# Three product widths in place of four in the expert stage of an attention, experts and MLP kernel

## The chip, the cores and the metric

The kernel runs on one core of a Trainium2 chip. The metric is the device time of one execution in microseconds (us), taken as the median of several executions. The profile is of one more execution of the same program.

## The reference

Three layers follow each other. What concerns the change is the second one, and of it the two matrix products per expert:

```python
def _moe_ref(x, expert_emb, tau, w1, w2):        # x: 2304 tokens x 512
    logits = xn @ en.T / tau                     # en: 8 experts
    expert_idx = np.argmax(logits, axis=1)
    ...
    for e in range(E):                           # E = 8
        mask = expert_idx == e
        h = np.maximum(x[mask] @ w1[e], 0.0)     # 512 -> 1024
        out[mask] = gate_w[mask, None] * (h @ w2[e])   # 1024 -> 512

def reference(...):
    attn_out = _attn_ref(q, k, v, w_phi)         # linear attention, 4 x 8 heads x 576 x 64
    x = _moe_ref(x=tokens of attn_out, ...)
    return _moe2_ref(x, w1, w2, w3, w_out)       # max of three products with 512 x 768, then 768 x 512
```

How many tokens an expert gets depends on the data, and differs from expert to expert. With these inputs the eight experts get 291, 494, 122, 198, 430, 296, 283 and 190 tokens.

## The kernel before

The kernel has three stages, one after the other on one core: the attention (until about 217 us of the profile), the experts (217.6 to 463.3 us) and the last MLP (from 463.3 us). All code is unrolled; each engine has one fixed sequence of instructions, written in the order in which the Python code issues them, and engines wait for each other through semaphores.

Attention ends with the routing (class `Routing`): each token's expert by an argmax, the tokens counted by expert (`ne`, line 732), and for each expert the number of the thresholds in `th` that its count exceeds (`cmp`, line 735, and the sum into `vi`). `th` is filled on GpSimd at line 658 from `WIDTHS` without its last entry. So `vi` holds for each expert the index of the smallest width that holds all its tokens. A count over `CAP` = 512 is dealt with by another path (`redo`), which these inputs jump over.

The experts stage (`Mlps.experts`) loops over the eight experts. Tokens stand as columns, sorted by expert, so an expert's tokens are a range of columns that starts at an offset known only at run time. The first product of an expert is cut into eight units (`A`, f = 0 to 7; line 987), each of 12 matmuls into one PSUM bank: four pieces of 128 input features, with three terms each, since inputs and weights are split into a high and a low part. The second is cut into four units (`B`, d = 0 to 3; line 1006) of 24 matmuls each. So an expert has 8 x 12 + 4 x 24 = 192 matmuls.

The number of columns of a matmul is fixed in its instruction. So each unit is written once for every width (`pick`, line 958 on): the index is in a register of TensorE (one load for each expert, line 1023), compare-and-branch instructions of TensorE's own sequencer (line 966) choose one of the copies, and the other copies are jumped over. `pick` halves the list of widths: with four, two compares choose. A width N multiplies the first N columns from the offset on; columns beyond the expert's own tokens are computed and later overwritten or left out.

With these counts the eight experts take the widths 304, 512, 224, 224, 448, 304, 304 and 224, in this order.

What the other engines do in a unit does not depend on the width: ScalarE and VectorE read 512 columns of the bank always (lines 994, 995 and 1009). Between the units they split the next expert's weights into high and low part (`split_w`; lines 849 and 854 for the first product, 957 and 958 for the second), after which SyncE loads the weights of a later expert into the same buffer (line 861). For expert 0 alone the first unit of `A` also brings in tokens (`first`): there ScalarE and VectorE branch too.

Of the kernel before, what the change touches and what calls it, by code (L numbers as in the profile page):

```python
# [617 lines left out]
class Routing:  # L618


    WIDTHS, CAP = (224, 304, 448, 512), 512

    def __init__(self, tc, gp, rp, NT, E):
        self.tc, self.nc, self.gp, self.rp = tc, tc.nc, gp, rp
# [780 lines left out]
```

## Time and profile before

| | |
|---|---|
| median of 3 runs | 770.54 us (770.53, 770.54 and 772.1) |
| the profiled execution | 771.95 us |
| its span, first to last instruction | 770.2 us |
| TensorE (PE) busy | 733.9 us, 95% |
| VectorE (DVE), ScalarE (ACT), GpSimd (POOL) busy | 403.9, 353.9 and 136.1 us |
| mean granted TensorE clock | 0.989 of 2.4 GHz |
| experts stage in the profile | 217.6 to 463.3 us |

The profile names work by engine and line of the code. A busy share is an average over stages with different limits. A row of the timeline ends, where the engine was idle before it, with the idle time in us and what ended it; "issue" there is time in which the engine waited for nothing that the profile shows. Branches, register loads and waits run on an engine's sequencer ("PEldq" for TensorE's), which runs ahead of the array, and don't count as busy. The queue "instruction" among the DMA queues carries the program's own code.

### The profile page before, as it was taken

How to read it: one execution, taken by the hardware profiler on the slowest of the kernel's cores; microseconds unless marked ns; L12 is line 12 of the kernel's file. 1: busy time of each engine (PE TensorE's matmuls, PEld its weight loads, DVE VectorE, ACT ScalarE, POOL GpSimd, SP SyncE). 2: the span in 40 equal slices, each digit the busy share in tenths (PEclk: the TensorE clock that was granted, in tenths of full speed). 3: DMA queues.
4: the chain of work that ended last, by engine and by line, in shares of the span. 5: the costliest groups of instructions: out<-in, count | busy, mean ns of one | idle time of the engine just before them, and what ended most of it. 6: DMA issues, size and time to landing. Idle time of an engine off the chain costs nothing. (4 is left out here: it accounts for less than half of the span.)

```text
span 770.2 us, 13409 instructions
## 1 busy us (share of the span) xinstructions
PE 733.9 (95%) x5492; PEld 607.6 (79%) x5492; DVE 403.9 (52%) x619; ACT 353.9 (46%) x600; POOL 136.1 (18%) x113
## 2 busy tenths in 40 slices
PE   8899999899998999898999998999999999999995
PEld 6566666665698889898999997888888887888884
DVE  7876666777765454484455678766522122212220
ACT  4676757676665445574455575343230131013111
POOL 1654223442151101004700000000020011002002
PEclk9899999999999999999999999999999999999999
DMA  9644433026248442454423605432010001001001
GB/s 202 141 102 99 115 89 83 18 83 221 81 131 302 162 168 80 172 170 116 162 108 118 220 9 164 161 119 102 2 54 28 1 23 36 0 1 56 0 1 55
DMA packets 59755, 76.15 MB, mean 99 GB/s; under 512 B 11632, under 2 KB 41976, under 8 KB 59648
## 3 DMA queue, kind: packets, MB, share of 16 engines
q1 hardware_dynamic: 55712, 64.53, 27.0%
q0 software_dynamic: 3456, 9.46, 3.6%
q8 instruction: 83, 1.36, 0.8%
q10 hardware_dynamic: 480, 0.61, 0.2%
q14 instruction: 24, 0.20, 0.1%
HBM read 65.12 MB, written 9.46 MB: 97 GB/s over the span
## 5 line engine op out<-in xcount | busy, mean ns | idle before, releaser
L1260 DVE TENSOR_TENSOR raw<-raw,b 128x512 f32<-128x512 f32 x36 | 24.8, 688 | 130.6 <-PE b L1252 126.8
L341 POOL PARTITION_ALL_REDUCE mq<-pq x32 | 69.0, 2207 | 98.0 <-ACT pq L339 91.3
L1006 PE MATMUL b<-hxH,wH 128*128 128x304 f32 (+3 forms) x256 | 80.1, 313 | 3.5 <-issue 3.5
L1281 POOL DMA_INDIRECT out_dram<-raw,c2t x18 | 17.8, 988 | 363.9 <-ACT raw L1280 334.5
L995 DVE SCALAR_TENSOR_TENSOR hxL<-b,hxH 128x512 fp32r<-128x512 f32 x64 | 42.4, 687 | 75.1 <-ACT hxH L994 74.8
L1006 PE MATMUL b<-hxL,wH 128*128 128x304 f32 (+3 forms) x256 | 79.4, 310 | 0.0
L1006 PE MATMUL b<-hxH,wL 128*128 128x304 f32 (+3 forms) x256 | 79.2, 309 | 0.0
L994 ACT ACTIVATE hxH<-b 128x512 fp32r<-128x512 f32 x64 | 38.4, 607 | 51.6 <-PE b L987 51.6
L987 PE MATMUL b<-xeH,w1lo 128*128 128x304 f32 (+3 forms) x256 | 56.8, 317 | 4.9 <-issue 4.9
L987 PE MATMUL b<-xeH,w1hi 128*128 128x304 f32 (+3 forms) x256 | 56.4, 313 | 0.0
L1006 PEld LDWEIGHTS b<-hxH,wH 128*128 128x128 f32 x256 | 48.4, 189 | 6.6 <-issue 4.9
L1006 PEld LDWEIGHTS b<-hxL,wH 128*128 128x128 f32 x256 | 48.5, 189 | 1.8
L1006 PEld LDWEIGHTS b<-hxH,wL 128*128 128x128 f32 x256 | 48.4, 189 | 1.7
L987 PEld LDWEIGHTS b<-xeH,w1lo 128*128 128x128 f32 x256 | 43.4, 195 | 7.5 <-issue 5.4
L987 PEld LDWEIGHTS b<-xeH,w1hi 128*128 128x128 f32 x256 | 42.0, 189 | 1.6
L958 DVE TENSOR_TENSOR wL<-raw,wH 128x2048 fp32r<-128x2048 f32 x16 | 36.7, 2294 | 11.4 <-ACT wH L957 11.4
L987 PE MATMUL b<-xeL,w1lo 128*128 128x304 f32 (+3 forms) x128 | 39.9, 316 | 0.0
L987 PE MATMUL b<-xeL,w1hi 128*128 128x304 f32 (+3 forms) x128 | 39.8, 311 | 0.0
L927 POOL DMA_INDIRECT xs<-x_d,s2t x18 | 21.9, 1215 | 101.3 <-PE b L933 71.1
L1264 ACT CAST m2h<-raw 128x512 fp32r<-128x512 f32 x12 | 7.4, 620 | 67.8 <-DVE raw L1260 67.8
L228 DVE TENSOR_REDUCE mk<-pskp 128x4 f32<-128x512 f32 x36 | 24.6, 684 | 24.9 <-PE pskp L217 24.9
L1009 ACT COPY xy<-b 128x512 f32 (+1 forms) x32 | 18.0, 587 | 42.1 <-PE b L1006 41.8
(254 smaller groups left out, 1786.7 us busy)
## 6 DMA issues: line engine op xcount, KB each, us to landing
raw<-in_moe_w_dram SPq DMA_DIRECT2D x32, 1024.0 KB, 5.8
raw<-in_moe_w_dram SPq DMA_DIRECT2D x18, 512.0 KB, 3.5
q<-in_q_dram SPq DMA_DIRECT2D x8, 576.0 KB
kv<-in_v_dram SPq DMA_DIRECT2D x8, 512.0 KB, 7.3
x_d<-x SPq DMA_DIRECT2D x16, 256.0 KB, 2.1
kv<-in_k_dram SPq DMA_DIRECT2D x7, 512.0 KB, 5.5
raw<-in_moe_w_out_dram SPq DMA_DIRECT2D x6, 512.0 KB, 4.8
kv<-in_k_dram SPq DMA_DIRECT2D x2, 256.0 KB
```

Of the source, the lines that this page charges most:

```text
L228: nc.vector.tensor_reduce(m, psb[j], axis=AX.X, op=ALU.max, apply_absolute_value=True)
L341: nc.gpsimd.partition_all_reduce(mx.rearrange("p a b -> p (a b)"), d.rearrange("p a b -> p (a b)"), P, ReduceOp.absmax)
L927: self.nc.gpsimd.indirect_dma_start(out=d, out_offset=None, in_=self.x_d, in_offset=bass.IndirectOffsetOnAxis(ap=idx, axis=0))
L958: self.nc.vector.tensor_tensor(L, r, H.bitcast(F32), op=ALU.subtract)
L987: nc.tensor.matmul(ps[:, 0:N], w, x[:, k, 0:N], start=(i == 0), stop=(i == 11))
L994: nc.scalar.activation(hH, ps, AF.Relu)
L995: nc.vector.scalar_tensor_tensor(hL, ps, 0.0, hH.bitcast(F32), op0=ALU.max, op1=ALU.subtract)
L1006: nc.tensor.matmul(ps[:, 0:N], w[i][:, c:c + P], h[f // 4][:, f % 4, 0:N], start=(f == 0 and q == 0), stop=(f == 7 and q == 2))
L1009: nc.scalar.copy(self.xy[:, d, bass.ds(o, 512)], ps)
L1260: nc.vector.tensor_tensor(m, m, b, op=ALU.max)
L1264: nc.scalar.copy(hH, m)
L1281: nc.gpsimd.indirect_dma_start(out=self.out, out_offset=bass.IndirectOffsetOnAxis(ap=rt.c2t[:, t:t + 1], axis=0), in_=o, in_offset=None)
```

## The change

One line: the width 448 is taken out of the list, and three widths are left.

```diff
 class Routing:
...
-    WIDTHS, CAP = (224, 304, 448, 512), 512
+    WIDTHS, CAP = (224, 304, 512), 512
```

Everything else follows from it. `th` has two thresholds in place of three (one small fill on GpSimd less, and `cmp` has 16 values in place of 24). Expert 4 (430 tokens) takes 512 columns in place of 448. `pick` halves three widths into one and two: one compare leads to 224, a second one tells 304 from 512.

On TensorE each unit loses one copy. This is the first unit of the second product of expert 0 in the program before (a unit of 24 matmuls; three of each copy shown, and b, hxH, hxL, wH, wL are the PSUM bank, the two parts of the hidden layer and of the weights):

```order
L966 COMPARE_AND_BRANCH x2
L1006 MATMUL b_2885<-hxH_2880,wH_2874 128x224
...
L966 UNCONDITIONAL_BRANCH
L1006 MATMUL b_2885<-hxH_2880,wH_2874 128x304
...
L966 UNCONDITIONAL_BRANCH
L966 COMPARE_AND_BRANCH
L1006 MATMUL b_2885<-hxH_2880,wH_2874 128x448
...
L966 UNCONDITIONAL_BRANCH
L1006 MATMUL b_2885<-hxH_2880,wH_2874 128x512
```

and in the changed program:

```order
L966 COMPARE_AND_BRANCH
L1006 MATMUL b_2884<-hxH_2879,wH_2873 128x224
...
L966 UNCONDITIONAL_BRANCH
L966 COMPARE_AND_BRANCH
L1006 MATMUL b_2884<-hxH_2879,wH_2873 128x304
...
L966 UNCONDITIONAL_BRANCH
L1006 MATMUL b_2884<-hxH_2879,wH_2873 128x512
```

Three copies of 24 matmuls stand in a row where four stood, with one compare and one jump less. The units of the first product change in the same way, with 12 matmuls a copy. The order of the work on the other engines is the same, but for one copy less of the two token blocks that ScalarE and VectorE bring in with expert 0.

## Rows read from the trace of the kernel before

**Rows 1.** Page: busy time of the engines; code queue (packets, MB, share).

```profile
PE 733.9 (95%) x5492; PEld 607.6 (79%) x5492; DVE 403.9 (52%) x619; ACT 353.9 (46%) x600; POOL 136.1 (18%) x113
...
q8 instruction: 83, 1.36, 0.8%
```

**Rows 2.** Busy time by stretch, one for each expert, in order.

```profile
core 0: us, PE busy (x) PEld busy (x) DVE busy (x) ACT busy (x) POOL busy (x), PEclk, DMA share, GB/s
217.60:249.10 31.50, 29.34 (x213) 28.81 (x213) 19.88 (x25) 19.56 (x27) 7.92 (x7) 1.00 0.63 222
249.10:294.70 45.60, 45.60 (x211) 37.67 (x210) 19.56 (x30) 18.23 (x23) 4.98 (x4) 1.00 0.42 150
294.70:319.20 24.50, 23.62 (x209) 23.26 (x208) 16.91 (x17) 17.93 (x24) 3.42 (x2) 1.00 0.44 160
319.20:349.10 29.90, 25.05 (x202) 24.25 (x200) 17.14 (x18) 17.35 (x22) 0.00 (x0) 0.94 0.50 172
349.10:388.10 39.00, 38.96 (x192) 36.14 (x193) 16.84 (x15) 15.63 (x18) 22.04 (x18) 1.00 0.36 113
388.10:414.60 26.50, 26.50 (x194) 26.49 (x193) 16.40 (x15) 15.95 (x19) 0.00 (x0) 1.00 0.41 147
...
441.10:463.30 22.20, 21.65 (x193) 21.48 (x193) 16.42 (x16) 14.69 (x17) 0.00 (x0) 1.00 0.13 44
```

**Rows 3.** TensorE's waits in the experts stage: us in total, times, longest.

```profile
PE b L987 <- issue: 4.9, 3, 2.3
PE b L1006 <- issue: 3.5, 6, 1.4
```

**Rows 4.** Timeline of TensorE: matmuls with idle time before them, and what ended it.

```profile
241.40 0.41 PE L1006 MATMUL b<-hxH,wH 128*128 128x304 f32 x1 [1.42 <-issue]
...
245.72 0.41 PE L1006 MATMUL b<-hxH,wH 128*128 128x304 f32 x1 [0.75 <-issue]
...
323.39 0.49 PE L987 MATMUL b<-xeH,w1lo 128*128 128x224 f32 x2 [2.34 <-issue]
...
340.96 0.36 PE L1006 MATMUL b<-hxH,wH 128*128 128x224 f32 x1 [0.20 <-issue]
...
344.15 0.36 PE L1006 MATMUL b<-hxH,wH 128*128 128x224 f32 x1 [0.26 <-issue]
...
349.14 0.46 PE L987 MATMUL b<-xeH,w1lo 128*128 128x448 f32 x1 [2.05 <-issue]
...
445.83 0.36 PE L987 MATMUL b<-xeH,w1lo 128*128 128x224 f32 x1 [0.55 <-issue]
```

**Rows 5.** Line 966 in the experts stage: duration in ns, least, median and longest.

```profile
L966 PEldq COMPARE_BRANCH  x274: 65/176/3571, 218.5 to 461.3; - x137
```

**Rows 6.** DMA: code queue (packets, MB, share), 217 to 464 us; GB/s of expert 0.

```profile
q8 instruction: 50, 0.82, 1.4%
...
GB/s 198 172 255 36 94 239 125 208 0 21 0 0 0 0 36 283 408 354 401 297 364 377 406 440 416 408 419 401 395 416 411 349 99 42 0 0 0 114 270 416
```

**Rows 7.** Line 1006 alone, in experts 1 (512 columns) and 4 (448 columns).

```profile
272.77:294.67 21.90, 21.90 (x96) 17.92 (x96) 1.00 0.31 111
368.69:388.14 19.45, 19.45 (x96) 17.84 (x95) 1.00 0.32 112
```

**Rows 8.** Busy time by stretch, as in rows 2, before and after the idle 2.34 us.

```profile
319.20:323.40 4.20, 1.86 (x18) 1.78 (x17) 0.69 (x1) 1.19 (x2) 0.00 (x0) 1.00 0.54 215
323.40:326.90 3.50, 3.50 (x18) 3.50 (x17) 0.69 (x1) 1.48 (x2) 0.00 (x0) 0.51 0.02 5
```

**Rows 9.** Timeline: the split of first-product weights; expert 1's first product.

```profile
245.97 1.23 DVE L854 TENSOR_TENSOR w1lo<-raw,w1lo 128x1024 fp32r<-128x1024 f32 x1
...
249.14 0.62 PE L987 MATMUL b<-xeH,w1lo 128*128 128x512 f32 x2
...
342.02 1.22 DVE L854 TENSOR_TENSOR w1lo<-raw,w1lo 128x1024 fp32r<-128x1024 f32 x1
```

**Rows 10.** Timeline of TensorE: the first wait in the last MLP.

```profile
470.83 0.50 PE L1252 MATMUL b<-xeH,w1lo 128*128 128x512 f32 x1 [1.86 <-ACT xy L1256]
```

## The prediction, made before the changed kernel ran

> **What bounds the kernel now.** I read the page first. TensorE (PE) is busy 733.9 of 770.2 us and its matmuls and weight loads are equal in number, so each product takes two instructions [rows 1]. The question is then what TensorE does in the experts stage, the only one whose instructions change. The stretches by expert say how long each takes: 31.5, 45.6, 24.5, 29.9, 39.0 and 26.5 us for experts 0 to 5, and 22.2 for expert 7 [rows 2]. From them comes the pace of a matmul with its weight load: expert 5 at 304 columns takes 26.50 / 192 = 138 ns, expert 7 at 224 columns 21.65 busy us / 192 = 113 ns. Experts 2 and 3 have the same 192 matmuls of 224 columns as expert 7, and 17 and 10 others beside them, yet take 24.5 and 29.9 us. The waits tell why: in the whole stage TensorE waits for no data worth naming, but nine times for "issue", 4.9 us before the first product and 3.5 us before the second, 8.4 us together [rows 3]. Seven of the nine are shown [rows 4]; the other two, at 310.14 and 313.77 us, are the rest, 0.9 us. Most lie in experts 2 and 3 and at the border to expert 4, the two largest are 2.34 and 2.05 us.
>
> What is it that "issue" hides? The reader should put the branches beside it. A compare-and-branch or jump of line 966 lasts 176 ns in the median and 65 at least, but 3571 at most [rows 5]: a branch that leads into code which hasn't come yet takes microseconds. The code queue brought 50 packets in the stage, 0.82 MB, so 16 KB each [rows 6]. The stage has 8 experts x (8 units x 12 + 4 units x 24) matmuls x 4 copies x 2 instructions = 12,288 instructions, 246 for each packet. So all four copies are fetched, those that are jumped over too, and a packet feeds 246 / 96 = 2.56 units of the first product or 246 / 192 = 1.28 of the second: in both 30.75 executed matmuls. At 224 columns that is 30.75 x 113 = 3.5 us of work per packet, at 304 columns 4.2 us. The stalls at 340.96 and 344.15 us, one unit apart [rows 4], show what a packet takes when the engine has to wait for each: 3.2 us. At 224 columns code arrives hardly faster than it is used up, and any packet that is late stops the engine. At 304 columns it stopped only where the weight loads keep the DMA engines at some 400 GB/s (227 to 243 us, [rows 6]): 1.42 and 0.75 us in expert 0, none in expert 5.
>
> **Part one: the 448-column expert at 512 columns.** Expert 4's second product took 19.45 us for 96 matmuls, 202.6 ns each; expert 1's, at 512 columns, 21.90 us for 96, 228.1 ns [rows 7]. The difference, 25.5 ns, times 192 matmuls is **+4.9 us**, all on the path, since expert 4 has no wait inside it. ScalarE and VectorE read 512 columns either way, and have idle time here (busy 15.6 and 16.8 of 39 us [rows 2]). The Trainium skill, "TensorE: Matmul & The Clock Gate", section "Back-to-back issue gap", gives a sustained spacing of about 81 ns at 128 and 131 ns at 512 columns; my estimate from that page is 50 / 384 ns per column, 1.6 us for this part, by which the sum below would come out 3.3 us lower. The rows differ (228 ns at 512), and they decide.
>
> **Part two: a quarter less code.** The stage has 9,216 instructions in place of 12,288, so at 246 a packet some 37 to 38 packets in place of 50. A packet then feeds 41 executed matmuls, not 30.75: 4.6 us at 224 columns, 5.7 us at 304. Against the 3.2 us that a packet takes this is a slack of 1.4 us where 0.3 us was. What goes is bounded from both sides. If each wait loses only what one packet now covers more (10.25 matmuls, 1.16 us at 224 and 1.41 us at 304), of the nine waits 0.01 + 1.18 + 0.89 = 2.1 us stay: 6.3 us are gained. If the slack adds up from packet to packet, as TensorE's sequencer runs ahead and stores it up, all 8.4 us are gained. I take 0.4 us as what stays, near the second end, because expert 5, with 4.2 us per packet, already shows no wait at all [rows 2], and the changed program has more than that everywhere: **-8.0 us**. A wait of 2 us or more can come back where a packet is held up behind weight loads; that is the other end, and I keep it for the range.
>
> **Part three: the clock.** After the 2.34 us wait the granted clock is 0.51 for 3.5 us, 1.2 GHz in place of 2.4 [rows 8]. In these 3.5 us 18 matmuls ran, which at 113 ns take 2.0 us: 1.5 us lost. The waits of 1.42, 2.05 and 1.86 us [rows 4, 10] were followed by no such drop (the stretch of expert 4 has 1.00 [rows 2]). If the longest wait shrinks below these, the drop goes too: **-1.5 us**.
>
> **Part four: branches and small things.** Three experts at 224 columns have 12 units each with one compare less, 36 in all. The sequencer runs ahead, and in expert 5, with 12 units to choose, no idle time shows, so I cost this at nothing; were that cover gone, it would be 36 x 65 ns = 2.3 us of gain. One small fill on GpSimd less and a shorter compare on VectorE lie far from the stage: nothing.
>
> **What is late next.** Faster products reach the next expert's weights sooner. Expert 1 would start 2.2 us earlier, at about 247.0 us; the low part of its second weight block is done at 245.97 + 1.23 = 247.2 us [rows 9], and the first matmul that reads it is the eighth, 7 x 228 ns = 1.6 us in. The margin is 1.4 us. Before expert 4 the same step ends at 343.2 us while TensorE came at 349.14; it depends on TensorE's own earlier steps and moves forward with them. The wait of 1.86 us at the start of the last MLP [rows 10] is for ScalarE, whose work there starts from expert 7's results and moves along too; it stays.
>
> **The sum.** 771.95 + 4.9 - 8.0 - 1.5 = 767.35 us against the profiled execution. That one is 1.4 us above the median of 770.54. Part of the difference may be waits for code that fell out shorter in the other runs, part lies elsewhere; I split it, and subtract 0.7: **766.6 us**, 0.5% below the median. Less or more than 1.5 us, 0.2%, is about what a measurement can tell from no change.
>
> **The rivals.** *Half of the waits stay* (chance 0.14). If packets are late mainly because weight loads hold them up, the waits are set by when loads run, not by how much code is asked for. For it: the waits of expert 0 under full DMA load. Against it: expert 5 loads weights too (147 GB/s on average [rows 2]) and doesn't wait. With 4.2 us and the clock drop kept: 771.95 + 4.9 - 4.2 = 772.65, less 0.7 to 1.4 for the median: 771.6, no change that can be told.
>
> *All of the waits stay, and the path only grows* (chance 0.05). The place is the same nine waits; the price is 4.9 us. It holds if a jump into the next packet always costs its fetch, however long ago the previous one came: then fewer packets mean fewer waits only by a quarter, 2.1 us at most, and the clock drop stays. The time is between 770.54 + 4.9 - 2.1 = 773.3 and 775.4. It decides slower from the point where less than 3.4 us of the 9.9 is regained. Against it: expert 5 jumps just as often and shows no idle time [rows 2]. The Trainium skill speaks for it in one sentence of "Runtime: NRT & Kernel Launch", section "Instruction fetch mechanics": crossing a block of code is "mostly hidden", so that less code would buy nothing and 4.9 us would be added, 775.4 us; the 8.4 us of "issue" disagree [rows 3]. The same section says that a branch out of the fetched window must wait for a fetch, and with that the longest branch, 3571 ns, agrees [rows 5].
>
> *The next weights are late* (chance 0.08). If expert 1's weights use up the margin of 1.4 us, the 2.2 us regained in expert 0 become a wait for data, at most 2.2 us: up to 768.8 us, still faster.
>
> **How the numbers follow.** My forecast holds with 0.73. Its own range: at the low end all waits go, and with them the whole 1.4 us, 771.95 + 4.9 - 8.4 - 1.5 - 1.4 = 765.5; a further 0.7 is kept for expert 0, whose 31.5 us less 2.2 us of waits are still 2.8 us more than expert 5's, not all of it in its 20 other matmuls. At the high end 2.1 us of waits stay and nothing of the 1.4 us goes: 769.05. To hold 8 in 10 the range reaches some way into the half-stays case: **764.8 to 769.8 us**. Faster by over 0.2% (below 769.0): 0.73 + 0.08 and a little of the first rival, 0.82. Within: 0.12. Slower (above 772.1): 0.06.
>
> **What would show it.** In the profile of the changed kernel: some 37 to 38 packets in the code queue in the stage and some 70 in all; "issue" before lines 987 and 1006 well under 2 us; no branch of line 966 much over 1.5 us in experts 2, 3 and 7; a granted clock of 1.00 in expert 3, and that expert near 24 us; expert 4 at 43.9 us with 192 matmuls of 512 columns; the last MLP as long as before. Four or more us of "issue" would prove the prediction wrong at part two, idle time at expert 1's start with VectorE as releaser at the margin, and an expert 4 much under 43 us at part one.

## The result and the profile after

The changed kernel takes 762.07 us in the median of six runs (759.82 to 766.39), beside 771.5 us for the kernel before in runs of the same chip (six, 770.53 to 776.88). The ratio is 0.987, with a 95% interval of 0.984 to 0.991. A later comparison with twelve runs gave 763.12 us against 771.66 us, 0.990 (0.988 to 0.993). So the change saves some 8 to 9 us, 1.0 to 1.3%. The direction was forecast, the size was not: the forecast was 766.6 us, in a range of 764.8 to 769.8.

The profiled execution of the changed kernel took 762.83 us with a span of 761.1 us; the one before took 771.95 and 770.2. The page shows the same work on TensorE and thirteen packets of code less [rows 1]:

```profile
PE 734.4 (96%) x5492; PEld 605.0 (79%) x5492; DVE 403.4 (53%) x619; ACT 353.4 (46%) x600; POOL 135.6 (18%) x112
...
q8 instruction: 70, 1.15, 0.7%
```

The stretches by expert answer to [rows 2]; the columns are the same:

```profile
216.90:245.70 28.80, 28.80 (x213) 28.80 (x214) 16.99 (x19) 17.37 (x24) 7.81 (x7) 1.00 0.63 220
245.70:291.20 45.50, 45.50 (x210) 37.61 (x210) 22.38 (x36) 20.32 (x27) 4.97 (x4) 1.00 0.46 163
291.20:314.30 23.10, 23.10 (x209) 23.10 (x208) 16.92 (x17) 16.59 (x22) 3.41 (x2) 1.00 0.43 144
314.30:336.70 22.40, 22.40 (x202) 22.33 (x202) 16.96 (x18) 17.76 (x24) 0.00 (x0) 1.00 0.55 192
336.70:380.30 43.60, 43.60 (x194) 36.09 (x194) 16.83 (x15) 16.31 (x19) 21.67 (x18) 1.00 0.44 132
380.30:406.80 26.50, 26.50 (x194) 26.48 (x193) 16.40 (x15) 15.96 (x19) 0.00 (x0) 1.00 0.43 148
...
433.20:455.10 21.90, 21.90 (x194) 21.56 (x193) 16.75 (x17) 14.56 (x17) 0.00 (x0) 1.00 0.15 52
```

In every stretch shown TensorE is busy from end to end. Against before, expert 0 is 2.7 us shorter, expert 1 0.1, expert 2 1.4, expert 3 7.5 and expert 7 0.3: 12.0 us together. Expert 4, now at 512 columns, is 4.6 us longer; expert 5 is the same. The stage takes 7.4 us less.

In the experts stage there is no row of "issue" at all, where [rows 3] had 8.4 us; the waits of TensorE that come next lie at the start of the last MLP (first fence below). Branches of nearly two microseconds still exist (line 966 in the whole program, compare [rows 5]), but no idle time stands behind them: the longest lasts from 319.04 to 320.94 us, and all through it TensorE works off matmuls of the units before. The code queue brings 37 packets in the stage (last fence), where [rows 6] had 50:

```profile
PE b L1252 <- ACT xy L1256: 1.4, 1, 1.4
PE b L1252 <- DVE xy L1260: 0.5, 1, 0.5
```

```profile
L966 PEldq COMPARE_BRANCH  x228: 70/176/1897, 213.6 to 453.2; - x114
```

```profile
q8 instruction: 37, 0.61, 1.2%
```

The other 1.6 us between the two spans lie outside the stage: 0.7 us before it, where the granted clock of the first 36 us was 0.95 in this execution and 0.91 in the earlier one, and 0.9 us after it, half of which is the wait for ScalarE, 1.38 us in place of 1.86 [rows 10]. The first of these differs from execution to execution: in a second profile of the changed kernel the clock of the first 36 us was 1.00, and the stage began at 214.6 us in place of 216.9.

### The profile page after: what moved, and what is told of

Read it like the earlier page. It is cut to its first block, busy times and chain, and to the rows that moved or that the text cites. A ratio compares the mean times of both kernels' runs of the same rounds, so it can differ in the third digit from the quotient of the medians.

```text
span 761.1 us, 13360 instructions
## 1 busy us (share of the span) xinstructions
PE 734.4 (96%) x5492; PEld 605.0 (79%) x5492; DVE 403.4 (53%) x619; ACT 353.4 (46%) x600; POOL 135.6 (18%) x112
## 5 line engine op out<-in xcount | busy, mean ns | idle before, releaser
L1006 PE MATMUL b<-hxH,wL 128*128 128x304 f32 (+2 forms) x256 | 80.3, 313 | 0.0
L1006 PE MATMUL b<-hxH,wH 128*128 128x304 f32 (+2 forms) x256 | 80.2, 313 | 0.0
L1006 PE MATMUL b<-hxL,wH 128*128 128x304 f32 (+2 forms) x256 | 80.0, 313 | 0.0
L987 PE MATMUL b<-xeH,w1hi 128*128 128x304 f32 (+2 forms) x256 | 57.2, 317 | 0.0
L987 PE MATMUL b<-xeH,w1lo 128*128 128x304 f32 (+2 forms) x256 | 55.7, 313 | 0.0
L987 PE MATMUL b<-xeL,w1hi 128*128 128x304 f32 (+2 forms) x128 | 40.1, 313 | 0.0
L987 PE MATMUL b<-xeL,w1lo 128*128 128x304 f32 (+2 forms) x128 | 39.5, 312 | 0.0
L1252 PE MATMUL b<-xeH,wH 128*128 128x512 f32 x96 | 37.3, 389 | 0.0
```

Source lines behind the costliest of these rows:

```text
L987: nc.tensor.matmul(ps[:, 0:N], w, x[:, k, 0:N], start=(i == 0), stop=(i == 11))
L1006: nc.tensor.matmul(ps[:, 0:N], w[i][:, c:c + P], h[f // 4][:, f % 4, 0:N], start=(f == 0 and q == 0), stop=(f == 7 and q == 2))
L1252: nc.tensor.matmul(b, w, y[k], start=(k == 0 and q == 0), stop=(k == 3 and q == 2))
```

## The experiments

Each run was timed against the kernel before on the same chip, whose median in these comparisons was 771.2 to 771.7 us.

**As much code as before, with the new columns.**

```diff
-    WIDTHS, CAP = (224, 304, 448, 512), 512
+    WIDTHS, CAP = (224, 304, 512, 512), 512
```

> Widths 224, 304, 512 and 512 again: the columns of the changed kernel, with as much code as before (the fourth copy is never run). If the gain is code that no longer has to be fetched, the nine waits of before come back and 512 columns still cost 4.6 us: 774 to 779 us, some 50 packets in the code queue in the experts stage, 'issue' of 5 us or more. If the gain comes from anything else that goes with three widths (columns, thresholds, VectorE's and ScalarE's shares), it stays near 762 us.

It took 776.03 us (ten runs, 772.45 to 778.39), 1.0054 of the kernel before (1.0032 to 1.0076). The code queue has 50 packets in the stage again, and the waits are back:

```profile
q8 instruction: 50, 0.82, 1.4%
...
PE b L987 <- issue: 5.0, 3, 2.9
PE b L1006 <- issue: 3.7, 5, 1.8
```

Expert 4 has the columns of the changed kernel here, and the copies, the packets and the compares are as many as before. So the new columns are not the gain: it goes with the fourth copy, be it by its code or by the compare that it adds to a unit of 224 columns. The run without weight loads below tells these two apart. The difference to the kernel before is the price of the wider expert, 4.2 us by these medians (2.5 to 5.9), 4.6 us by the stretches above.

**A quarter more code, with the old columns.**

```diff
-    WIDTHS, CAP = (224, 304, 448, 512), 512
+    WIDTHS, CAP = (224, 304, 384, 448, 512), 512
```

> Widths 224, 304, 384, 448 and 512: every expert takes the columns of before, with a quarter more code. A packet then feeds 24.6 matmuls, 2.8 us at 224 columns, less than the 3.2 us that a packet takes when it is waited for. If code supply sets the waits, they grow to 20 us or more in the experts stage: 783 to 800 us. If the waits depend on the number of branches or on the weight loads alone, the time stays within 770 to 775 us.

It took 797.66 us (793.27 to 802.77), 1.0356 (1.0308 to 1.0404). No expert has between 304 and 384 tokens, so the fifth copy is never run, and it costs 26 us. There are 63 packets in the stage, and "issue" adds up to 20.6 us:

```profile
q8 instruction: 63, 1.03, 1.6%
...
PE b L987 <- issue: 12.3, 7, 3.3
PE b L1006 <- issue: 4.8, 7, 1.8
PE b L933 <- issue: 3.5, 1, 3.5
```

Dead code costs what it delays, and the cost is far from proportional: 13 packets more cost 26 us, 13 less save some 12.

**Half the code.**

```diff
-    WIDTHS, CAP = (224, 304, 512), 512
+    WIDTHS, CAP = (304, 512), 512
```

> Widths 304 and 512: two copies of each unit, half the code of before, and the three experts that ran at 224 columns run at 304: 3 x 192 x 25 ns = 14.4 us more matmul time. If the changed kernel has no wait for code left, there is nothing further to regain: 762 + 14.4 = 776 to 777 us. If some of its time is still lost to code, 774 us or less.

It took 776.55 us (774.24 to 777.99), as expected. Its stage lasts 252.8 us in the profile, 14.5 more than the changed kernel's 238.3, as much as its three experts at 304 columns need. No branch of line 966 lasts over 0.35 us any more, and that brings nothing further:

```profile
L966 PEldq COMPARE_BRANCH  x168: 70/174/348, 213.3 to 466.0; - x168
```

So with three copies the supply of code is no longer on the path.

**The kernel before without weight loads.** This run leaves out the loads of the weights of experts 2 to 7, so that these experts are computed with the weights of expert 1.

```diff
-                    if e + 1 < E:
+                    if e == 0:
                         ex.load(2 + f // 2, e + 1)
...
-                    if e + 2 < E:
-                        ex.load(i, e + 2)
-                    else:
+                    if e + 2 >= E:
                         self.load_m2(i)
```

> The kernel before, but the weights of experts 2 to 7 are never loaded (expert 1's are used again): the experts stage without 24 of its weight transfers, with the same code. If packets are late because weight transfers hold them up, 'issue' falls from 8.4 to under 3 us and the time to about 762 us. If the plain rate of the code queue sets the waits, 'issue' stays above 6 us and the time above 768 us.

It took 765.2 us (763.69 to 767.44), 0.9912 (0.9884 to 0.994). "Issue" is halved, not gone:

```profile
PE b L987 <- issue: 2.3, 2, 2.0
PE b L1006 <- issue: 2.1, 3, 1.5
```

The 1.5 us wait, with one of 0.4 us after it, lies in expert 0, beside which expert 1's weights are still loaded (242.56 us; 1.42 us at 241.40 before [rows 4]). The 2.0 us wait lies at 350.59 us, in expert 4, and is followed by a clock of 0.50. Within experts 2 and 3 only 0.2 us is left, and 0.3 at the border to expert 4, where 2.05 was. So four copies of code would nearly have sufficed, had nothing else moved; it takes both the code and the loads beside it. My expectation of under 3 us was missed (4.4), and the time lies 3 us over the 762 that I gave; the places speak for the loads. How a load makes a packet late stays open: the transfers of the code packets take 1.1 us each on average with the loads and without them (1.4% of 16 engines over 247 us for 50 packets [rows 6]; 1.5% over 248 us for 52 here).

This run also settles what a compare costs. Expert 2's second product has four copies here and two compares in each unit; with no wait in it, it takes as long as in the changed kernel with three copies and one compare, 10.79 us:

```profile
307.84:318.63 10.79, 10.79 (x100) 10.79 (x97) 8.45 (x9) 7.10 (x9) 0.00 (x0) 1.00 0.11 30
```

So the compares are free here, and what the fourth copy costs it costs by its code.

**Four widths in one product, three in the other.** `pick` gets the list of widths as an argument; in these runs one product gets `(224, 304, 512)` and the other all four.

```diff
-    def pick(self, idx, unit, lo=0, hi=None):
-        W = self.rt.WIDTHS
+    def pick(self, idx, unit, lo=0, hi=None, W=None):
+        W = W or self.rt.WIDTHS
...
-        self.pick(idx, unit) if idx is not None else unit(512)
+        self.pick(idx, unit, W=(224, 304, 512)) if idx is not None else unit(512)
```

With three in the second product:

> Four widths in the first product, three in the second: a unit of the first product has the code of before, one of the second that of the changed kernel; expert 4 runs its first product at 448 columns and its second at 512, so half of the 4.6 us is saved. If a packet must be matched with the work that it feeds, the waits of the second product go and some of those of the first stay: 762 to 768 us. If waits of the first product stay as long as before (4.9 us and their overlap), 768 us or more.

It took 764.02 us (762.66 to 772.36), as expected, with 1.8 us of "issue". What expert 4's first product saves at 448 columns, the waits take back: no better than the changed kernel, within the spread. With three in the first product:

> Three widths in the first product, four in the second: the counterpart of the run with four and three. If each packet must be matched with the work that it feeds, the waits before the second product come back (3.5 us of idle and 1.5 to 2 us of overlap lost in six waits) and those before the first go: 762 + 5 - 2.3 = 764 to 766 us. If waits belong to the first product and the border between experts, it falls to 760 us.

It took 773.73 us (768.44 to 776.25), some 8 us over what I expected. That is 1.0028 of the kernel before (1.0001 to 1.0054), although that one has more code; it has 2.3 us less matmul time in expert 4. The waits of this run are 9.4 us:

```profile
PE b L1006 <- issue: 4.7, 7, 1.3
PE b L987 <- issue: 4.5, 2, 2.5
PE b L933 <- issue: 0.2, 1, 0.2
```

After the two longest of them the granted clock fell too: its mean was 0.87 in the 13.3 us from 320.48 us on and 0.94 in expert 4's first product, a further part of the 8 us. By my count of matmuls per packet the two runs should have differed little: the executed 224-column work per packet is 3.5 us in either product with four copies. What differs is what else moves. In this run the stretch of expert 2's first product and that of its second read:

```profile
293.32:305.69 12.37, 12.37 (x114) 12.37 (x112) 8.46 (x9) 9.53 (x14) 3.41 (x2) 1.00 0.28 96
305.69:320.48 14.79, 11.46 (x100) 10.93 (x97) 8.45 (x9) 8.97 (x12) 0.00 (x0) 1.00 0.66 242
```

The last two columns are the share of the DMA engines and GB/s: the next weights are loaded mainly beside the second product, 242 GB/s against 96. So I took the loads out of this run too, in the same way as above:

> The run with three widths in the first and four in the second product, without the weight loads of experts 2 to 7. The weight loads run mainly beside the second product, and the waits of that run lie in it and right after it. If it is the weight loads beside the four-copy second product that make packets late, its waits in experts 2 to 4 (some 10 us with the clock's share) go: about 763 us. If four copies of 24 matmuls are too much code whatever else moves, it stays above 770 us.

It took 765.33 us (760.33 to 768.76), 8.4 us less, but 2 us over what I expected: of the 2.6 us of "issue" that are left, 2.0 lie in expert 0, where expert 1's weights still come. The same two stretches are

```profile
294.56:306.93 12.37, 12.37 (x114) 12.37 (x112) 8.46 (x9) 9.53 (x14) 3.41 (x2) 1.00 0.08 24
306.93:317.72 10.79, 10.79 (x100) 10.79 (x98) 8.46 (x9) 7.09 (x9) 0.00 (x0) 1.00 0.11 30
```

The second product of expert 2 falls from 14.79 to 10.79 us, with the same code, and the loads are what was taken away. So the second product's fourth copy is the dear one because its code must come while the weights come; the counterpart, loads moved beside the first product, was not tried.

**Second profiles.** The kernel before, once more:

> The kernel before once more, unchanged, for a second profile. If the waits depend on when packets land among other transfers, their places and sizes differ from the first profile, with a sum between 6 and 12 us of 'issue' in the experts stage; if they are fixed by the code alone, the same nine places and 8.4 us come again.

It took 770.08 us in its one run. Its waits in the stage are

```profile
PE b L1006 <- issue: 3.6, 5, 1.8
PE b L987 <- issue: 3.0, 2, 2.3
PE b L987 <- ACT xy L1009: 1.4, 1, 1.4
PE b L1006 <- ACT xeH L946: 0.3, 1, 0.3
PE b L987 <- ACT hxH L994: 0.3, 1, 0.3
```

All nine places of the first profile are there again with other sizes: 1.81 and 0.37 us in expert 0 where 1.42 and 0.75 were, and 1.36 at the border to expert 4 where 2.05 was; the one at 344.15 us shrank to 0.10. Two are new, 0.3 us each in expert 3, where the first profile had half the clock instead after its wait of 2.34 us. The last three rows bear ScalarE's name. The wait at the border was "issue" in the first profile and goes with the code, so the name beside a wait need not be its cause; whether the two new ones are waits for code too is not shown. So the places come mostly from the code, and the sizes differ from execution to execution. Each half of my expectation held in part: the sum of "issue", 6.6 us, lies in the range, but the places did not move. The changed kernel once more:

> The changed kernel once more, for a second profile and for a comparison on one chip with the run at 496 columns: 760 to 764 us, and again no 'issue' before lines 987 and 1006 if the slack per packet is what counts; one or two waits of up to 1 us if the first profile was a lucky one.

It took 763.12 us (760.61 to 765.71) and has no "issue" in the stage again, which lasts 238.3 us in both profiles. So the first profile was not an exception.

**A smaller largest width.**

```diff
-    WIDTHS, CAP = (224, 304, 512), 512
+    WIDTHS, CAP = (224, 304, 496), 496
```

> The changed kernel with 496 in place of 512 as its largest width (494 is the largest count; more than 496 tokens would go the other path): the same code, and 16 columns less in the 384 matmuls of experts 1 and 4. At the 0.38 to 0.4 ns per column that 448 against 512 gave (24 to 25.5 ns for 64), 384 x 16 x 0.39 = 2.4 us less: 759 to 760 us. If the weight load sets the pace and not the columns, no change from 762 us.

It took 763.05 us (757.93 to 764.3), which is no gain by the medians. Expert 4's second product takes 21.44 us for 96 matmuls in its profile, 223 ns each, where the changed kernel takes 21.76 us, 227 ns:

```profile
353.97:375.41 21.44, 21.44 (x96) 17.88 (x95) 1.00 0.31 100
```

That is 4 ns x 384 = 1.5 us less for the two experts, and the stage lasts 236.8 us where the changed kernel's lasts 238.3. So a matmul's time does go by its columns, and not by the weight load alone. Beside the changed kernel on the same chip:

> The kernel with 496 as its largest width once more, beside the changed kernel: the first profile shows 223 ns for a matmul where 512 columns take 227, so 384 x 4 = 1.5 us less than the changed kernel. If that is real the medians differ by 1 to 2 us; the spread of single runs is larger than that, so it may not show.

This time it took 761.17 us against 763.12, 0.988 of the kernel before (0.984 to 0.993) against 0.990 (0.988 to 0.993). The intervals overlap, so whether this version beats the changed one in the time of a whole execution stays open; it also sends counts of 497 to 512, which the changed kernel holds, the other path.

## Why the prediction was wrong

**What bounds the kernel** was read rightly. Waits for code are what "issue" hid: with the columns of the changed kernel a fourth copy brings them back, and with the columns of before a fifth multiplies them. One figure in it was less sure than it looked. The 3.2 us that a packet takes came from two waits one unit apart; a unit is 24 matmuls, while a packet feeds 30.75, so this spacing is not the time of a packet. The transfers alone take 1.1 us each, and the rest, from the request on, was not measured. The run with five copies, 2.8 us of work per packet, agrees with 3.2, but doesn't measure it. The sentence of the Trainium skill, "Runtime: NRT & Kernel Launch", section "Instruction fetch mechanics", that crossing a block of code is mostly hidden, holds in the changed kernel and not in the one before, nor in the run with five copies.

**Part one** (+4.9 us) was nearly right: 4.6 us, since 512 columns took 227 ns and not 228 in expert 4. My estimate of 1.6 us from the Trainium skill's "TensorE: Matmul & The Clock Gate", section "Back-to-back issue gap", does not agree with this.

**Part two** (-8.0 us) is the step that failed, and it was the size of its term. I took the idle time in front of the waiting matmuls, 8.4 us, as all that there was to gain. The stretches show 12.0 us regained; without the clock's share of 1.5 us that is 10.5. The idle time counts from the end of the matmul before, and matmuls overlap: each lasts longer than the pace at which they follow each other. Two places in the timeline of the kernel before show it:

```profile
312.80 0.28 PE L1006 MATMUL b<-hxL,wH 128*128 128x224 f32 x1
313.77 0.36 PE L1006 MATMUL b<-hxH,wH 128*128 128x224 f32 x1 [0.70 <-issue]
313.97 0.28 PE L1006 MATMUL b<-hxH,wL 128*128 128x224 f32 x1
314.08 0.27 PE L1006 MATMUL b<-hxL,wH 128*128 128x224 f32 x1
...
346.81 0.28 PE L1006 MATMUL b<-hxL,wH 128*128 128x224 f32 x1
349.14 0.66 PE L987 MATMUL b<-xeH,w1lo 128*128 128x448 f32 x2 [2.05 <-issue]
```

From 312.80 to 313.77 us are 0.97 us from start to start, where 0.11 is the pace: 0.86 us lost, of which 0.70 are marked idle. The next start comes after 0.20 us, not 0.11: 0.09 more. From 346.81 to 349.14 us 2.33 us pass, 2.22 more than the pace, for 2.05 marked. So a wait costs some 0.16 us more than its idle time, and 0.09 after it. Over all nine the starts lie 9.9 us further apart than the pace, and with what follows each wait it is 10.7 us, beside the 10.5 that the stretches show. Nothing of it stayed, where I kept 0.4. So of the two bounds the one at which all waits go was right; that it is because "the slack adds up from packet to packet" fits, but no run singles it out.

**Part three** (-1.5 us) went as forecast: the clock is 1.00 in expert 3 now, and the 18 matmuls at half the clock are gone.

**Part four and what is late next** held. The compares cost nothing, as the run without weight loads shows. There is no wait for weights at expert 1 or expert 4, but the margin of 1.4 us before expert 1 was overestimated: in the two profiles of the changed kernel 0.5 and 0.9 us are left between the end of the split and the matmul that reads it. The wait in front of the last MLP did not stay quite as it was, but that is no gain of its own: from expert 7's first matmul of the second product to the end of that wait 18.2 us pass in both profiles, which ScalarE and VectorE set.

**The median.** I subtracted 0.7 us for the difference between the profiled execution and three runs. With more runs the kernel before has a median of 771.2 to 771.7 us, so there was little to subtract. The stage lasted 245.7 and 245.3 us in its two profiles, so the change is worth 7 to 7.4 us there; what the medians show beyond that, 1 to 2 us, is about the size of the 1.6 us outside the stage, of which I can say where it lies but not that the change makes it.

Added up on the profiled executions: 767.35 forecast against 762.83, 4.5 us. Of these 2.5 are part two, 0.3 part one, 0.7 lie before the stage and 0.9 after it. With parts one and two at their measured sizes the forecast would have been 763.8 us, already under the range, against the 762.07 measured.

**The rivals.** That half of the waits stay because loads hold packets up named a true cause with the wrong result: without the loads of experts 2 to 7 half of the "issue" goes, yet with three copies all of it goes although the loads stay. That all waits stay fell with the first profile.

**What was to be seen** came true for the packets (37 in the stage, 70 in all), the clock, expert 4 (43.6 us for 43.9) and "issue". The longest branch was forecast at not much over 1.5 us and was 1.9 us, without effect.

## What to carry to other kernels

Code that is jumped over is fetched all the same: count what an engine executes per packet of the code queue against what a packet takes to come, at the busiest moment of the other transfers, before a further variant of an unrolled body is added. Here 3.5 us of work per packet was too little beside some 220 to 240 GB/s of loads, 4.6 us was enough, and with 2.8 us the kernel became 26 us slower. Read what a wait costs from start to start of the instructions around it, not from the idle time alone.

## What the hardware showed that I had not expected

The clock after a wait is not a matter of its length alone. In the first profile of the kernel before, the 2.34 us wait at 323.39 us was followed by a granted clock of 0.51 [rows 8]. In its second profile a 2.33 us wait ended at the same matmul, at 322.69 us, and the clock stayed at its higher level:

```profile
322.70:326.20 3.50, 3.50 (x32) 3.50 (x32) 0.69 (x1) 2.31 (x3) 0.00 (x0) 1.00 0.02 5
```

32 matmuls ran in 3.5 us here, and 18 there. In the run without weight loads 1.97 us of wait was enough for a clock of 0.50.

That wait, at 350.59 us, came with no weight load on the way. The code packet before it was slow itself: between 342.77 and 347.87 us one code packet was on the way all the time (first line below: 6.2% of 16 engines is one engine), 5.1 us where 1.1 is the mean. What ran beside it in the same stretch (342 to 355 us, the other two lines) were 1,271 packets of together 0.01 MB, which by their size are the small write of the gates. The changed kernel has a code packet of 5.7 us at its own gates, from 341.17 us on, and no wait after it. That the small packets held the code up is argued from their place; leaving them out was not tried.

```profile
q8 instruction: 1, 0.02, 6.2%
...
q1 hardware_dynamic: 1271, 0.01, 5.1%
q8 instruction: 3, 0.05, 3.7%
```
